# Rows of 1/rms written and spread from ScalarE's queue, and group 0's q in halves

## The chip, the cores and the metric

The kernel runs on one core of a Trainium2 chip. A core has five engines that run beside each other: TensorE (PE, with its weight loads listed apart as PEld), VectorE (DVE), ScalarE (ACT), GpSimd (POOL) and SyncE (SP). SyncE computes nothing here; it issues DMA transfers. ScalarE and GpSimd can issue them too. Each engine works through its own instructions in the order of the program, and waits where an instruction needs the result of another engine or of a transfer.

The metric is the device time of one execution in microseconds (us). Before the change its median was 531.6 us over 3 runs (530.16 to 532.11). The execution that the profiler recorded has a span of 526.9 us, and all times of single instructions below are counted from the start of that span.

## What is computed

There are two blocks. The first is attention with q and k normalised by their root mean square (8 batches, 12 heads, 448 tokens, 64 elements of a head):

```
q_n = q / sqrt(mean(q*q) + 1e-6) * g_q          # k likewise with g_k
attn = softmax(q_n @ k_n.T / 8);  x = attn @ v
```

The heads are put side by side, so that x has 448 rows of 768 elements in each batch. The second block scores each token by x @ w_gate, takes the 128 best of each batch, runs them through a layer of 1024 (w1, relu, w2), and adds the result, weighted by a sigmoid of the score, to those rows of x.

## The kernel before

**Groups and units.** Four heads of one batch make a group: two pairs c of two heads hh. There are 24 groups, n = 0 to 23, three to a batch. A group's 448 keys are cut into 7 blocks of 64; a group and a block make a unit, 168 in all, so units 7n to 7n + 6 belong to group n. For each unit PE multiplies keys by queries (`scores`, L289), ScalarE takes the exponential (L298), with 1/rms of the keys as its scale, one number for each partition, and PE multiplies the result by v (`values`, L313). DVE and, in the first six groups, GpSimd too add the exponentials up over the blocks (`add_probs`, L329 and L335); PE sums those over the keys (L367) and turns them (L392); DVE inverts them (L394), and PE turns the attention's result to tokens (L410), which DVE scales (L412).

**Where q is normalised.** The queries lie along the free dimension of the scores' right operand qT. So 1/rms of the queries has to be a row, the same on the 64 partitions of a head, before DVE can multiply qT by it (`scale_q`, L248). The way there for group n is:
- `squares` (L207) on ScalarE and `sum_squares` (L214 on DVE, then the power of -1/2 at L217 on GpSimd) give rinv, 14 numbers on each of 128 partitions;
- `rows_out` (L228) writes rinv to DRAM as two rows of 896 numbers, one row for each hh;
- `rows_in` (L239) reads each row back to 64 partitions of the tile bc (two buffers); a partition gets 3584 bytes, and the whole of bc is 448 KB;
- `scale_q` multiplies qT by bc and by the product of the two gains.

Before the change SyncE issues all three transfers, between its loads of q, k, v and weights and its stores of x. The first two groups do not go through DRAM: `scale_q_early` (L260, L268) spreads rinv with small matmuls on PE into two PSUM banks and multiplies from there. The scores have four banks in all, of the same pool.

**What sets the order.** The program lists the work of the engines by hand. A step q has four units. It lists the scores, exponentials and values of its units first, then the work given to its slots 4q to 4q + 3 in two halves, with pieces of the second block and other tasks between the halves. Each engine thus finds its part of a slot behind its part of that step's units. SyncE has no part in the units, and so reaches its slots as early as its own waits allow. `prepare(n, slot)` (L658) gives slots to the way of group n's rows: squares and sums in slot to slot + 3, `rows_out` at slot + 6 or + 7, `rows_in` at slot + 8, + 9 or + 10. Slot is 7n - 20 from group 6 on, and at most 7n - 17 before (0 for group 2, 4 for group 3). `scale_q` is in slot 11 for group 2, 15 for group 3, and from then on 7n - 6.

**The beginning.** `Loads.__init__` issues the first loads (two of tok, one of qT) ahead of a branch that picks this program. tok holds the token-major copies from which squares are taken: for each group one for q and one for k, in loads of 448 KB. While the first of them is on its way, PE does 26 transposes of the identity (L164) whose results nobody reads.

Of the kernel before, what the change touches and what calls it, by code (L numbers as in the profile page):

```python
# [10 lines left out]
F32 = mybir.dt.float32  # L11
I32 = mybir.dt.int32
AF = mybir.ActivationFunctionType
OP = mybir.AluOpType
# [11 lines left out]
class Loads:  # L26


    def __init__(self, nc, pool, qT, kT, vp, tok, g2):
        self.nc, self.pool = nc, pool  # L30
        self.src = {"tok": tok, "qT": qT, "kT": kT, "v": vp}
        self.tiles = {}
        self.groups = tok.shape[1]
        self.gcol = pool.tile([128, 2], F32, name="gcol", bufs=1)
        nc.scalar.dma_start(out=self.gcol, in_=g2)
        neg_half = pool.tile([128, 1], F32, name="neg_half", bufs=1)
        nc.vector.memset(neg_half, -0.5)

        warm = pool.tile([128, 1], F32, name="warm", bufs=1)
        nc.scalar.activation(out=warm, in_=neg_half, func=AF.Exp)  # L40
        self.neg_half = neg_half
        self.load("tok", 0, 0)
        self.load("tok", 0, 1)
        self.load("qT", 0)

    def load(self, name, n, i=None):
        b, g = divmod(n, self.groups)
        src = self.src[name]
        if i is not None:
            src = src[b, g, :, i]  # L50
        elif name == "v":
            src = src[b, g]
        else:
            src = src[b, 2 * g : 2 * g + 2].rearrange("c p s -> p c s")
        pool = self.v_pool if name == "v" else self.pool
        bufs = {"tok": 6, "qT": 4, "kT": 3, "v": 3}[name]
        held = [key for key in self.tiles if key[0] == name]
        if len(held) == bufs:
            del self.tiles[held[0]]
        t = pool.tile(list(src.shape), F32, name=name, bufs=bufs)  # L60
        self.nc.sync.dma_start(out=t, in_=src)
        self.tiles[name, n, i] = t

    def get(self, name, n, i=None):
        return self.tiles[name, n, i]
# [3 lines left out]
def fast(  # L69
# [21 lines left out]
    nc = tc.nc  # L91

    B, NP, _, S = loads.src["qT"].shape
    CP = 112
    NJ = S // CP
    D = 64
    NI = S // D
# [14 lines left out]
    norm_pool = ctx.enter_context(tc.tile_pool(name="norm", bufs=2))  # L112
# [7 lines left out]
    ps_sc = ctx.enter_context(tc.tile_pool(name="ps_sc", bufs=4, space=PSUM))  # L120
# [20 lines left out]
    load, get, neg_half = loads.load, loads.get, loads.neg_half  # L141

    ident = const.tile([128, 128], F32, name="ident")
# [12 lines left out]
    for c in range(2):  # L156
        nc.vector.memset(pick_pair[D * c : D * (c + 1), c : c + 1], 1.0)
    nc.vector.scalar_tensor_tensor(
        out=gg, in0=loads.gcol[:, 0:1], scalar=scale, in1=loads.gcol[:, 1:2], op0=OP.mult, op1=OP.mult
    )  # L160

    ps = ps_moe.tile([128, 512], F32, tag="moe", name="warm_ps")
    for _ in range(26):
        nc.tensor.transpose(out=ps[:, 0:128], in_=ident, identity=ident)  # L164

    wg = const.tile([CP, DM], F32, name="wg")
# [36 lines left out]
    def squares(n, i):  # L203
        t = get("tok", n, i)
        sq = sqs[(2 * n + i) % 2]
        for h in [slice(0, 1), slice(1, 2)] if (n, i) == (0, 0) else [slice(0, 2)]:
            nc.scalar.activation(out=sq[:, h, :, 0:D], in_=t[:, h], func=AF.Square, scale=scale)  # L207
        sss[n, i] = norm_pool.tile([128, 2, NI], F32, name="ss", bufs=4)
        return sq

    def sum_squares(n, i, sq):
        ss = sss.pop((n, i))
        for h in [slice(0, 1), slice(1, 2)] if (n, i) == (0, 0) else [slice(0, 2)]:
            nc.vector.tensor_reduce(out=ss[:, h], in_=sq[:, h], axis=AX.X, op=OP.add)  # L214
        rinv = norm_pool.tile([128, 2, NI], F32, name="rinv", bufs=8)
        flat = "p h i -> p (h i)"
        nc.gpsimd.tensor_tensor(  # L217
            out=rinv.rearrange(flat),
            in0=ss.rearrange(flat),
            in1=neg_half.to_broadcast([128, 2 * NI]),  # L220
            op=OP.pow,
        )
        rinvs[n, i] = rinv

    def rows_out(n):

        rows = dram_pool.tile([2, 2 * S], F32, name="rows", bufs=3)
        nc.sync.dma_start(  # L228
            out=rows.rearrange("h (p i) -> p h i", i=NI), in_=rinvs.pop((n, 0))
        )  # L230
        bcs[n] = rows

    def rows_in(n):

        rows = bcs[n]
        bc = norm_pool.tile([128, 2, S], F32, name="bc")
        for hh in range(2):
            src = rows[hh].rearrange("(c s) -> c s", c=2)
            nc.sync.dma_start(  # L239
                out=bc[D * hh : D * (hh + 1)],  # L240
                in_=dataclasses.replace(src, ap=[[0, D]] + [list(x) for x in src.ap]),
            )
        bcs[n] = bc

    def scale_q(n):
# [6 lines left out]
    def scale_q_early(n):  # L252

        rinv = rinvs.pop((n, 0))
        for c in range(2):
            ps = ps_sc.tile([128, 512], F32, tag="sc", name="sc")
            r = slice(D * c, D * (c + 1))
            for i in range(NI):
                for hh in range(2):
                    nc.tensor.matmul(  # L260
                        out=ps[D * hh : D * (hh + 1), D * i : D * (i + 1)],
                        lhsT=rinv[r, hh, i : i + 1].to_broadcast([D, D]),
                        rhs=ident[r, r],
                        start=True,
                        stop=True,
                    )
            t = get("qT", n)[:, c].rearrange("d (p i) -> d p i", i=NI)
            nc.vector.scalar_tensor_tensor(  # L268
                out=t,
                in0=t,  # L270
                scalar=gg,
                in1=ps[:, 0:S].rearrange("d (i p) -> d p i", i=NI),
                op0=OP.mult,
                op1=OP.mult,
            )
# [145 lines left out]
    gates, parts, rowss, highers, ranks, slots_dram = {}, {}, {}, {}, {}, {}  # L421
# [212 lines left out]
    def at(slot, fn, *args):  # L634
        todo.setdefault(slot, []).append(lambda: fn(*args))
# [22 lines left out]
    def prepare(n, slot):  # L658
        sq = {}
        for i in range(2):  # L660
            at(slot + 2 * i, lambda i=i: sq.setdefault(i, squares(n, i)))
            at(slot + 2 * i + 1, lambda i=i: sum_squares(n, i, sq.pop(i)))

        at(slot + (7 if n > 2 else 6), rows_out, n)
        at(slot + (10 if n > 5 else 9 if n > 2 else 8), rows_in, n)

    for n in range(1, n_groups):
        s0 = NI * n
        if n > 2:
            at(max(s0 - 26, 4 * (n - 3)), load, "tok", n, 0)  # L670
            at(max(s0 - 26, 4 * (n - 3)), load, "tok", n, 1)
        if n > 1:
            at(max(s0 - 13, 2), load, "qT", n)
            at(max(s0 - 11, 2), load, "kT", n)
            at(max(s0 - 11, 2), load, "v", n)
            first = max(s0 - (20 if n > 5 else 17), 0)
            prepare(n, first)
            at(max(s0 - 6, first + 11), scale_q, n)
# [73 lines left out]
    for i in range(2):  # L752
        sum_squares(0, i, squares(0, i))
# [515 lines left out]
def _build(nc, ap, cap, out):  # L1269
    D = ap["g_q"].shape[0]  # L1270
    with tile.TileContext(nc) as tc, ExitStack() as ctx:
        load_pool = ctx.enter_context(tc.tile_pool(name="load", bufs=1))
        with tc.tile_pool(name="bound", bufs=1) as pool:
            g = pool.tile([1, 2, D], F32, name="g")
            nc.sync.dma_start(out=g, in_=ap["g_row"])
            loads = Loads(nc, load_pool, *(ap[n] for n in ("qT", "kT", "vp", "tok", "g2")))


            prod = pool.tile([1, D], F32, name="prod")
            nc.vector.tensor_mul(out=prod, in0=g[:, 0], in1=g[:, 1])  # L1280
            nc.vector.tensor_mul(out=prod, in0=prod, in1=prod)
            top = pool.tile([1, 1], F32, name="top")
            nc.vector.tensor_reduce(out=top, in_=prod, axis=AX.X, op=OP.max)
            small = pool.tile([1, 1], I32, name="small")
            nc.vector.tensor_scalar(
                out=small,
                in0=top,
                scalar1=MAX_SCORE * MAX_SCORE / D,
                scalar2=None,
                op0=OP.is_le,  # L1290
            )
            is_small = nc.values_load(small[0:1, 0:1], min_val=0, max_val=1,
                skip_runtime_bounds_check_because="a comparison gives 0 or 1")
        with tc.If(is_small > 0) as cmp, tc.manual_schedule():
            fast(
                tc, loads, *(ap[n] for n in _INS[5:]), cap, out,
            )
        with cmp.Else():
            general(tc, *(ap[n] for n in _INS), cap, out)
# [45 lines left out]
```

## Time and profile before

| | before |
|---|---|
| time, median of 3 (us) | 531.6 (530.16 to 532.11) |
| span of the profiled execution (us) | 526.9 |
| PE busy | 507.6 us, 96% |
| DVE busy | 334.2 us, 63% |
| ACT busy | 278.1 us, 53% |
| POOL busy | 191.8 us, 36% |
| rows_out: issues, median us from issue to landing | 22 of 7 KB, 5.4 |
| rows_in: issues, median us from issue to landing | 44 of 224 KB, 6.4 |
| DVE waiting for bc | 5.1 us, 3 times |

A line of the timeline has the start and the length in us, the engine (SPq and ACTq for the queue of issues), the line of the kernel, the operation, and out<-in by the program's names; what stands in brackets at its end is how long the engine had been idle before, and what ended that. In the chain of work that ended last each piece has its start, its length, and the engine or transfer that filled it. The busy time of an engine is a mean over stages that differ: ScalarE, for instance, is busy for 15.2 of the 20 us from 40 to 60, and for 57.2 of the 100 us from 150 to 250. A transfer's landing is the time at which its last part has arrived; an issue is the instruction that starts it.

### The profile page before, as it was taken

What the parts mean: (1) busy time and instruction counts of PE and PEld (TensorE: products, weight loads), DVE (VectorE), ACT (ScalarE), POOL (GpSimd) and SP (SyncE); (2) the same over time, 40 slices, a digit from 0 to 9 for tenths busy, and PEclk for the clock granted to TensorE, in tenths of its full rate; (3) what the DMA queues carried; (4) which work ended last, traced back from release to release, by engine and by line L of the source; (5) the groups of instructions that cost most, each with busy time, mean ns of one, the idle gap of its engine ahead of it and who ended that gap; (6) DMA issues with size and microseconds to landing.
All of it is one profiled execution on the core that took longest, in us unless ns stands there. A gap on an engine that the chain in (4) does not pass through costs nothing.

```text
span 526.9 us, 11121 instructions
## 1 busy us (share of the span) xinstructions
PE 507.6 (96%) x4482; PEld 298.8 (57%) x4482; DVE 334.2 (63%) x638; ACT 278.1 (53%) x507; POOL 191.8 (36%) x109
## 2 busy tenths in 40 slices
PE   6999997999999999999999999998999999999995
PEld 5544343565744476546654467644664448659694
DVE  4566879579846896658666787467947487336101
ACT  4886873857644845456644585645463474401100
POOL 4956866623512454132712424304621003002102
PEclk9999998999999999999999999999999999999998
DMA  8968779799764297526846396537542231104100
GB/s 304 382 217 291 244 224 345 251 291 340 200 187 161 82 291 232 163 94 192 260 136 183 87 297 211 159 103 223 195 131 71 70 136 31 31 1 143 53 32 35
DMA packets 43405, 93.21 MB, mean 177 GB/s; under 512 B 11059, under 2 KB 23348, under 8 KB 43346
## 3 DMA queue, kind: packets, MB, share of 16 engines
q1 hardware_dynamic: 39938, 86.11, 52.1%
q0 software_dynamic: 3264, 6.31, 3.5%
q8 instruction: 37, 0.61, 0.5%
q14 instruction: 22, 0.18, 0.1%
q10 hardware_dynamic: 144, 0.00, 0.0%
HBM read 74.93 MB, written 25.35 MB: 190 GB/s over the span
## 4 chain that ended last, share of the span: by engine, by line
PE 89%; DVE 4%; DMA 2%; ACT 2%; issue 2%; POOL 0%; DVEq 0%; SPq 0%; ACTq 0%; POOLq 0%
PE sc L289 24%; PE av L313 22%; PE moe_ps L575 13%; PE moe_ps L595 11%; PE sc L595 4%; PE x_ps L410 4%; PE sc L575 4%; PE den_ps L367 3%; DMA bc<-rows 2%; PE denT_ps L392 1%; ACT p L298 1%; DVE sum L335 1%; PE warm_ps L164 1%; DVE ss L214 1%; DVE x L412 1%
## 5 line engine op out<-in xcount | busy, mean ns | idle before, releaser
L298 ACT ACTIVATE p<-sc,rinv 128x448 f32<-128x448 f32 x336 | 186.6, 642 | 106.3 <-PE sc L289 92.5
L217 POOL TENSOR_TENSOR rinv<-ss,neg_half 128x14 f32<-128x14 f32 x48 | 128.8, 2689 | 198.3 <-DVE ss L214 170.6
L289 PE MATMUL sc<-qT,kT 64*64 64x448 f32 x1344 | 154.8, 549 | 1.1 <-DVE qT L268 0.4
L313 PE MATMUL av<-p,v 64*64 64x448 f32 x1344 | 147.1, 537 | 0.0
L335 DVE TENSOR_TENSOR sum<-sum,p 128x896 f32<-128x896 f32 x101 | 111.6, 1105 | 7.2 <-ACT p L298 0.9
L313 PEld LDWEIGHTS av<-p,v 64*64 64x64 f32 x1344 | 60.1, 133 | 67.6 <-issue 56.9
L289 PEld LDWEIGHTS sc<-qT,kT 64*64 64x64 f32 x1344 | 54.3, 133 | 70.9 <-issue 47.0
L214 DVE TENSOR_REDUCE ss<-sq 128x14 f32<-128x910 f32 (+1 forms) x49 | 52.4, 1074 | 33.9 <-ACT sq L207 33.9
L575 PE MATMUL moe_ps<-xeT,w 128*128 128x128 f32 x576 | 69.3, 277 | 0.0
L575 PEld LDWEIGHTS moe_ps<-xeT,w 128*128 128x128 f32 x576 | 66.2, 192 | 5.3 <-issue 5.3
L595 PE MATMUL moe_ps<-w,hT 128*128 128x384 f32 x176 | 61.3, 491 | 0.4 <-DVE xe L604 0.3
L412 DVE TENSOR_TENSOR x<-x_ps,rden 112x512 f32<-112x512 f32 x48 | 32.8, 690 | 37.2 <-PE x_ps L410 36.4
L506 POOL DMA_INDIRECT selected<-x,rank x32 | 33.6, 1050 | 47.3 <-DVE x L498 39.3
L207 ACT ACTIVATE sq<-tok 128x896 f32<-128x896 f32 (+1 forms) x49 | 46.4, 951 | 5.7 <-DMA tok<-in_tok_dram 3.7
L595 PEld LDWEIGHTS moe_ps<-w,hT 128*128 128x128 f32 x176 | 31.7, 190 | 22.5 <-issue 2.5
L436 DVE SCALAR_TENSOR_TENSOR prod<-x,wg 112x256 f32<-112x256 f32 x96 | 41.5, 432 | 3.0
L614 POOL DMA_INDIRECT out_dram<-xe,row x10 | 11.6, 1164 | 81.1 <-DVE rden L394 47.3
L410 PE MATMUL x_ps<-ident,xT 128*112 128x128 f32 x192 | 29.5, 279 | 3.3 <-DVE rden L394 3.3
L335 DVE TENSOR_TENSOR sum<-p 128x896 f32<-128x896 f32 x24 | 25.9, 1078 | 5.2 <-ACT p L298 5.2
L604 DVE SCALAR_TENSOR_TENSOR xe<-sc,xe 128x384 f32<-128x384 f32 (+1 forms) x6 | 3.3, 550 | 40.6 <-PE sc L595 40.6
L410 PEld LDWEIGHTS x_ps<-ident,xT 128*112 128x112 f32 x192 | 21.8, 135 | 12.6 <-issue 7.7
L248 DVE SCALAR_TENSOR_TENSOR qT<-qT,gg,bc 128x896 f32<-128x896 f32 x22 | 25.2, 1147 | 5.1 <-DMA bc<-rows 5.1
(71 smaller groups left out, 311.0 us busy)
## 6 DMA issues: line engine op xcount, KB each, us to landing
tok<-in_tok_dram SPq DMA_DIRECT2D x48, 448.0 KB, 6.3
qT<-in_qT_dram SPq DMA_DIRECT2D x24, 448.0 KB, 6.2
kT<-in_kT_dram SPq DMA_DIRECT2D x24, 448.0 KB, 7.0
v<-in_vp_dram SPq DMA_DIRECT2D x24, 448.0 KB, 7.7
out_dram<-x SPq DMA_DIRECT2D x8, 1344.0 KB, 7.8
bc<-rows SPq DMA_DIRECT2D x44, 224.0 KB, 6.4
xe<-selected SPq DMA_DIRECT2D x8, 385.0 KB, 3.1
w<-in_moe_w_dram SPq DMA_DIRECT2D x6, 512.0 KB, 6.4
```

The costliest lines, as they stand in the source:

```text
L207: nc.scalar.activation(out=sq[:, h, :, 0:D], in_=t[:, h], func=AF.Square, scale=scale)
L214: nc.vector.tensor_reduce(out=ss[:, h], in_=sq[:, h], axis=AX.X, op=OP.add)
L217: nc.gpsimd.tensor_tensor(out=rinv.rearrange(flat), in0=ss.rearrange(flat), in1=neg_half.to_broadcast([128, 2 * NI]), op=OP.pow,)
L289: nc.tensor.matmul(out=scs[hh][D * c : D * (c + 1), 0:S], lhsT=get("kT", n)[r, c, D * i : D * (i + 1)], rhs=get("qT", n)[r, c, :], start=True,
L298: nc.scalar.activation(out=p[:, hh], in_=scs[hh][:, 0:S], func=AF.Exp, scale=rinvs[n, 1][:, hh, i : i + 1],)
L313: nc.tensor.matmul(out=avs[n][c][D * hh : D * (hh + 1), 0:S], lhsT=get("v", n)[r, hh, i, :], rhs=probs[u][r, hh], start=(i == 0), stop=(i ...
L335: nc.vector.tensor_tensor(out=sums[n], in0=probs.pop(u - 1) if begins else sums[n], in1=probs.pop(u), op=OP.add)
L410: nc.tensor.transpose(out=ps[:CP, j, :], in_=t[:, j, :], identity=ident)
L412: nc.vector.tensor_tensor(out=xs[b][:, :, col : col + 128].rearrange("p j (h d) -> p j h d", d=D), in0=ps[:CP].rearrange("p j (h d) -> p j ...
L436: nc.vector.scalar_tensor_tensor(out=prod, in0=xs[b][:, j, cols], scalar=1.0, in1=wg[:, cols], op0=OP.mult, op1=OP.mult, accum_out=gates[b ...
L575: nc.tensor.matmul(out=ps[:, 128 * i : 128 * i + n], lhsT=w1[:, dc, 128 * (f0 + i) : 128 * (f0 + i + 1)], rhs=xeT[:, dc, :n], start=(dc == 0),
L595: nc.tensor.matmul(out=ps[:n, :width], lhsT=hT[:, fc, :n], rhs=w2[:, fc, cols], start=(fc == 0), stop=(fc == NFC - 1),)
```

## The change

Three things change.

1. `rows_out` and `rows_in` are issued by ScalarE in the place of SyncE, which keeps its queue for the loads and stores. `rows_in` becomes one transfer over both rows in the place of two over one row each. The slots become slot + 6 and slot + 8 for all groups.
2. For group 0's q, the load of tok is cut into two halves by hh, and so is the power at L217; squares and sums were in halves already. `scale_q_early` takes two banks at once and spreads all of hh = 0 first, then all of hh = 1, so that PE can begin with the first half.
3. The warm-up transposes go down from 26 to 11, for the spreading to start earlier.

```diff
-        self.load("tok", 0, 0)
+        self.load("tok", 0, 0, parts=2)
...
-        self.nc.sync.dma_start(out=t, in_=src)
+        w = src.shape[1] // parts
+        for part in range(parts):
+            cols = slice(w * part, w * (part + 1))
+            self.nc.sync.dma_start(out=t[:, cols], in_=src[:, cols])
...
-    for _ in range(26):
+    for _ in range(11):
...
         for h in [slice(0, 1), slice(1, 2)] if (n, i) == (0, 0) else [slice(0, 2)]:
             nc.vector.tensor_reduce(out=ss[:, h], in_=sq[:, h], axis=AX.X, op=OP.add)
-        nc.gpsimd.tensor_tensor(
-            out=rinv.rearrange(flat),
-            in0=ss.rearrange(flat),
-            in1=neg_half.to_broadcast([128, 2 * NI]),
-            op=OP.pow,
-        )
+            nc.gpsimd.tensor_tensor(
+                out=rinv[:, h].rearrange(flat),
+                in0=ss[:, h].rearrange(flat),
+                in1=neg_half.to_broadcast([128, (h.stop - h.start) * NI]),
+                op=OP.pow,
+            )
...
-        nc.sync.dma_start(
+        nc.scalar.dma_start(
             out=rows.rearrange("h (p i) -> p h i", i=NI), in_=rinvs.pop((n, 0))
         )
...
-        for hh in range(2):
-            src = rows[hh].rearrange("(c s) -> c s", c=2)
-            nc.sync.dma_start(
-                out=bc[D * hh : D * (hh + 1)],
-                in_=dataclasses.replace(src, ap=[[0, D]] + [list(x) for x in src.ap]),
-            )
+        (h_step, _), row = [list(x) for x in rows.ap]
+        nc.scalar.dma_start(
+            out=bc.rearrange("d c s -> d (c s)"),
+            in_=dataclasses.replace(rows[:, :], ap=[[h_step, 2], [0, D], row]),
+        )
...
-        for c in range(2):
-            ps = ps_sc.tile([128, 512], F32, tag="sc", name="sc")
-            r = slice(D * c, D * (c + 1))
-            for i in range(NI):
-                for hh in range(2):
+        spreads = [ps_sc.tile([128, 512], F32, tag="sc", name="sc") for _ in range(2)]
+        for hh in range(2):
+            for c, i in [(c, i) for i in range(NI) for c in range(2)]:
+                r = slice(D * c, D * (c + 1))
...
-        at(slot + (7 if n > 2 else 6), rows_out, n)
-        at(slot + (10 if n > 5 else 9 if n > 2 else 8), rows_in, n)
+        at(slot + 6, rows_out, n)
+        at(slot + 8, rows_in, n)
```

More of the change, by code (lines that the diff above doesn't have):

```diff
@@ L41, in __init__, with load @@
         self.neg_half = neg_half
-        self.load("tok", 0, 0)
+        self.load("tok", 0, 0, parts=2)
         self.load("tok", 0, 1)
         self.load("qT", 0)
-    def load(self, name, n, i=None):
+    def load(self, name, n, i=None, parts=1):
         b, g = divmod(n, self.groups)
@@ L212, in sum_squares @@
         ss = sss.pop((n, i))
+        rinv = norm_pool.tile([128, 2, NI], F32, name="rinv", bufs=8)
+        flat = "p h i -> p (h i)"
         for h in [slice(0, 1), slice(1, 2)] if (n, i) == (0, 0) else [slice(0, 2)]:
             nc.vector.tensor_reduce(out=ss[:, h], in_=sq[:, h], axis=AX.X, op=OP.add)
-        rinv = norm_pool.tile([128, 2, NI], F32, name="rinv", bufs=8)
-        flat = "p h i -> p (h i)"
-        nc.gpsimd.tensor_tensor(
-            out=rinv.rearrange(flat),
-            in0=ss.rearrange(flat),
-            in1=neg_half.to_broadcast([128, 2 * NI]),
-            op=OP.pow,
-        )
+            nc.gpsimd.tensor_tensor(
[4 more added lines that the diff above has]
+            )
         rinvs[n, i] = rinv
@@ L254, in scale_q_early @@
         rinv = rinvs.pop((n, 0))
-        for c in range(2):
-            ps = ps_sc.tile([128, 512], F32, tag="sc", name="sc")
-            r = slice(D * c, D * (c + 1))
-            for i in range(NI):
-                for hh in range(2):
[L260 to L266, printed above, removed]
+        spreads = [ps_sc.tile([128, 512], F32, tag="sc", name="sc") for _ in range(2)]
+        for hh in range(2):
+            for c, i in [(c, i) for i in range(NI) for c in range(2)]:
+                r = slice(D * c, D * (c + 1))
+                nc.tensor.matmul(
+                    out=spreads[c][D * hh : D * (hh + 1), D * i : D * (i + 1)],
+                    lhsT=rinv[r, hh, i : i + 1].to_broadcast([D, D]),
+                    rhs=ident[r, r],
+                    start=True,
+                    stop=True,
+                )
+        for c in range(2):
             t = get("qT", n)[:, c].rearrange("d (p i) -> d p i", i=NI)
@@ L271, in scale_q_early @@
                 scalar=gg,
-                in1=ps[:, 0:S].rearrange("d (i p) -> d p i", i=NI),
+                in1=spreads[c][:, 0:S].rearrange("d (i p) -> d p i", i=NI),
                 op0=OP.mult,
```

## The prediction

> **What bounds the kernel now.** I read the page's engine shares first, then the chain, then the stretches, and last the order of time on each queue in the first 100 us.
>
> ```profile
> PE 507.6 (96%) x4482; PEld 298.8 (57%) x4482; DVE 334.2 (63%) x638; ACT 278.1 (53%) x507; POOL 191.8 (36%) x109
> PE 89%; DVE 4%; DMA 2%; ACT 2%; issue 2%; POOL 0%; DVEq 0%; SPq 0%; ACTq 0%; POOLq 0%
> ```
>
> TensorE (PE) is busy for 96% of the span, so the change can remove little: the idle 19 us of PE, and time at a low clock. It can add much: any wait that reaches PE. The stretches (columns: window, length, busy us of PE, PEld, DVE, ACT, POOL, then granted clock, DMA share, GB/s) say where:
>
> ```profile
> 10.00:20.00 10.00, 9.82 (x162) 5.28 (x156) 4.66 (x6) 8.22 (x12) 8.61 (x4) 1.00 1.04 397
> 30.00:40.00 10.00, 10.00 (x115) 4.47 (x115) 6.04 (x4) 7.51 (x15) 6.18 (x3) 1.00 0.78 258
> 80.00:100.00 20.00, 16.50 (x162) 7.34 (x158) 14.49 (x30) 11.22 (x21) 13.80 (x8) 0.91 0.88 291
> 150.00:250.00 100.00, 99.72 (x860) 55.44 (x852) 72.54 (x132) 57.17 (x105) 32.06 (x15) 1.00 0.55 167
> ```
>
> From 10 to 20 us the DMA engines are full (share 1.04). From 30 to 40 PE never rests. Between 80 and 100 it loses 3.5 us and runs at 0.91 of its clock. From 150 on it loses almost nothing. The chain and the order of time name what fills the gap after 80:
>
> ```profile
> 34.98 1.67 PE sc L289 x16
> ...
> 71.35 7.98 DMA bc<-rows
> ...
> 87.26 1.10 PE x_ps L410 x4
> 88.36 2.78 PE sc L289 x16
> ```
>
> The broadcast bc of group 5, queued on SyncE behind a 1344 KB store of out, lands at 79.3. VectorE (DVE) waits 2.35 us for it, the reciprocals of L394 come late, and PE waits 3.27 us at 83.99. Then 16 score matmuls take 2.78 us; at 34.98 as many took 1.67.
>
> The broadcast of group 2 has the least room:
>
> ```profile
> 27.83 1.17 SPq L239 DMA_DIRECT2D bc<-rows  x2
> 31.00 2.29 ACT L298 ACTIVATE p<-sc,rinv 128x448 f32<-128x448 f32 x4
> 32.07 1.15 DVE L248 SCALAR_TENSOR_TENSOR qT<-qT,gg,bc 128x896 f32<-128x896 f32 x1 [2.48 <-DMA bc<-rows]
> 37.96 1.68 PE L289 MATMUL sc<-qT,kT 64*64 64x448 f32 x16
> 41.55 0.26 DVE L394 RECIPROCAL rden<-denT_ps 112x16 f32<-112x16 f32 x1 [3.13 <-PE denT_ps L392]
> ```
>
> It is issued at 27.83 and landed by 32.0; the 16 scores at 37.96 are units 14 and 15, the first of group 2, and read that qT. So 4.7 us separate the end of the multiply (33.2) from its reader.
>
> [...] The old broadcast counts 64 on both sides[...]. The new source pattern is [[h_step, 2], [0, 64], row]: its slowest dimension is 2, the destination's is 128[...]. No run of before has such a pattern. [...] In the trace of before ScalarE's ring carries one 1 KB load. [...] 2.78 against 1.67 us after 3.27 us of idling.
>
> **The change, part by part.**
>
> *First q in halves, pow in halves, 11 warm-ups.* The first tok lands at 4.54 and the first squares run at 4.64. A half can land some 0.7 us earlier, but the memsets that the squares also need end at 4.1, so I take 0.4. The pow of 14 columns takes 2.60 us; its half lies between 1.3 (in proportion) and 2.6 (all fixed). I take 1.4, since an add of 896 columns takes 2.08 on the same engine and so the fixed part is small. Together the last of group 0's pow moves from 9.1 to about 8.2, and the first scores from 11.39 to some 10.3. The warm-ups (26 in 4.97 us, 0.21 each while cold) then end near 7.0, and the first half's spreading fills the hole, so I charge nothing for the clock. But this gain is lost at 20 us: the tok of group 2 that ScalarE squares at 17.62 lands at 17.54, the DMA engines being full, and behind it come the sum (18.68) and the multiplies of L268 (19.70), which free the PSUM banks that the scores of 20.42 need. Those times stay. I take 0 here (ends: 0 and -1.1).
>
> *Issue costs on ScalarE.* 44 issues of 0.4 to 0.5 us (SyncE's: 0.38 and 0.50) come to some 20 us of its queue. From 150 us on ACT is busy 57 of 100 us and its gap between two steps' exponentials is 3.6 to 8 us, so they hide there, as does the wait of rows_in for rows_out. Before that the issue is done while the exponentials already queued still run. I take 0 to 2, value 0.5.
>
> *Moved from SyncE to ScalarE.* SyncE runs ahead of the compute; ScalarE issues in program order, behind the four units' exponentials of its step. Group 2's rows_in is in slot 8, after the exponentials of units 8 to 11, which start at 31.00 and end at 33.3. So it issues near 32.3, not at 27.83.
>
> *One broadcast in the place of two.* [...] At full share the 16 engines moved 397/1.04 = 382 GB/s, 23.9 each: 9.6 us. With the 1.8 us that the tiny ScalarE load of gcol took to land, 11.4 us is the lower end. [...] For group 2, SyncE's loads issued by 31.7 land until 38.3, so some 5 us of their work is in the way: I take 16. The old pair landed within 4.2.
>
> *Group 2:* landed 32.3 + 16 = 48.3, multiplied by 49.5; PE reached it at 38.0: a wait of 11.5 us (6.9 to 16.5), and 1.7 for the clock at half rate over 3.4 us. Sum 13.2. Queued behind the waiting multiply on DVE are three sums (33.14 to 38.4) and L394; DVE idled 3.13 before L394, so they add little.
>
> *Group 3:* rows_in is behind the exponentials of unit 15 (41.3), now near 54.9; landed at about 70. DVE reaches its multiply at 46.94 + 13.2 = 60.1 and waits 10. Behind it is the work up to the sums of 57.04 that PE awaited at 58.19, with only 1.6 us of idling. PE loses 7 (4 to 13).
>
> *Later groups:* group 4's rows_in and multiply lie a whole step apart, which is enough, but its rows_out stands behind the long broadcast on the ring while ScalarE waits for it; this falls in the same time as group 3's wait. Group 5's late broadcast stays as late as now: 68.5 + 12 is 80.5, against 79.3. From group 8 on there are six slots, 11 to 20 us, between rows_in and the multiply; 12 to 16 us fit or miss by little. I take 1.5 for all (ends -3 and +10).
>
> Sum: 0 + 0.5 + 13.2 + 7 + 1.5 = 22, over most of which nothing else is on the path. Hence **about 553 us**.
>
> **The rivals.**
>
> *Two engines, little sharing* (every broadcast in 11.4 us): group 2 costs 6.9 + 1.7, group 3 about 3, the rest nothing: 531.6 + 11.6 = 543. For it: while PE stands still SyncE's loads wait for buffers, so the ring empties. Against: 0.78 and 0.85 share in those stretches.
>
> *Sixteen engines, faster.* If the pattern is spread as the old one was, a broadcast lands in 4 to 5 us. Group 2 is then multiplied by about 38, just in time; group 5's is issued at 68.5, ahead of the store, and DVE gets its 2.35 us back, PE is never cold after 84 (1.76 us: 1.1 on the scores, 0.65 on L410): 531.6 - 4.1 = 527.5. For it: this is the only wait for bc that the chain shows. Against: the leading 2 of the pattern.
>
> *Sixteen engines, but ScalarE waits.* rows_out and rows_in of groups 4, 5 and 6 fall in one step, and ScalarE would wait 2 to 3.5 us for the landing before the next exponentials; PE catches 1 to 2 us of each of three. It cancels the gain: 531.6 - 4.1 + 5 = 532.5.
>
> **How the numbers follow.** Two engines with sharing 0.64, two engines with little 0.22, sixteen and faster 0.08, sixteen and no change 0.06. The likeliest gives 553. The range takes both two-engine cases with their bounds, 538 to 568, and leaves out the two others and a tail. Slower by over 0.5%: both two-engine cases, 0.86. Faster 0.08, same 0.06.
>
> **What would show each step right or wrong.** The landing of bc: 11 us or more says two engines, under 6 sixteen. Then DVE's wait before L248 in groups 2 and 3 (2.48 and 0 now): 10 us or more each; a PE gap of 7 to 16 us near 38 us, a slice with PEclk near 5 after it, and another near 60. The scores of 20.42 should stay within 0.5 us. The stretch from 150 us on should be as long as now; if it is not, waits of ScalarE for its own issues reach PE, and I have placed the cost wrongly. [...]

## The result, and the profile after

The changed kernel takes 598.23 us (594.84 to 599.23, 4 runs), the kernel before 530.88 us (530.03 to 532.11, 4 runs) on the same chip: a ratio of 1.1255, with a 95% interval of 1.1204 to 1.1307. It is 67 us slower where 22 were predicted, and outside the range. The profiled span is 596.6 us against 526.9, 69.7 more.

The lines of the page on the engines' shares and on the chain that ended last, changed kernel:

```profile
PE 524.2 (88%) x4467; PEld 304.8 (51%) x4467; DVE 330.9 (55%) x638; ACT 279.5 (47%) x507; POOL 191.9 (32%) x110
PEclk9997798799598999998999999899999999999999
PE 49%; DVE 2%; DMA 1%; issue 1%; ACT 1%; POOL 0%; ACTq 0%; POOLq 0%; DVEq 0%
```

PE fell from 96% to 88% of the span, and is busy 16.6 us longer with the same work: slices of PEclk stand at 5, 7 and 8, and the mean granted clock is 0.954, where it was 0.994. The chain's shares add up to 54% only, because it could be followed back from the end no further than to 267.9 us; so I read the stretches and the waits in place of it. The stretches, with the columns of before and one window more:

```profile
10.00:20.00 10.00, 8.46 (x112) 4.32 (x112) 3.90 (x5) 7.32 (x12) 8.99 (x4) 1.00 1.04 399
30.00:40.00 10.00, 8.65 (x95) 3.55 (x91) 0.10 (x1) 7.19 (x14) 6.35 (x3) 1.00 0.72 237
40.00:60.00 20.00, 10.28 (x94) 4.57 (x98) 9.18 (x16) 6.10 (x12) 2.85 (x2) 0.74 0.26 78
80.00:100.00 20.00, 16.34 (x162) 7.16 (x158) 11.86 (x23) 12.90 (x23) 12.86 (x6) 0.91 0.60 195
150.00:250.00 100.00, 89.94 (x760) 53.97 (x761) 67.78 (x126) 52.85 (x95) 30.92 (x15) 0.92 0.51 167
```

From 40 to 60 us PE is idle for half of the time and runs at 0.74 of its clock, while the DMA engines, taken together, are busy for a quarter of it (0.26): a transfer is awaited, and bandwidth is not what it lacks. From 150 to 250 us PE loses 10 us, where it lost 0.28 before. The waits, changed kernel (engine and line that waits, what ended the wait, us in all, times, longest):

```profile
DVE qT L250 <- DMA bc<-rows: 71.3, 9, 18.1
PE sc L291 <- ACT p L300: 32.7, 9, 12.0
ACT sq L210 <- DMA bc<-rows: 13.2, 1, 13.2
```

DVE waited 5.1 us for bc before. PE waiting for exponentials, the second line, was not among the waits of before at all. Group 2 in the order of time, changed kernel:

```profile
31.98 1.10 ACTq L241 DMA_DIRECT2D bc<-rows  x1
...
48.24 1.15 DVE L250 SCALAR_TENSOR_TENSOR qT<-qT,gg,bc 128x896 f32<-128x896 f32 x1 [18.14 <-DMA bc<-rows]
...
49.49 3.26 PE L291 MATMUL sc<-qT,kT 64*64 64x448 f32 x16 [10.84 <-issue]
...
54.87 0.26 DVE L396 RECIPROCAL rden<-denT_ps 112x16 f32<-112x16 f32 x1 [2.09 <-PE denT_ps L394]
```

The broadcast is issued at 31.98, and the multiply that reads it starts at 48.24: 16.3 us, where the old pair landed within 4.2. PE stands for 10.84 us and then takes 3.26 us for scores that took 1.68. The granted clock is 1.00 until 42.82 us, 0.50 from there to 53.06 and 1.00 again to 60.

The second kind of loss, at group 6. ScalarE's order of time, changed kernel:

```profile
103.07 0.36 ACTq L231 DMA_DIRECT2D rows<-rinv  x1
103.49 0.21 ACT L472 ACTIVATE parts<-parts 112x8 f32<-112x8 f32 x1
103.60 0.94 ACT L210 ACTIVATE sq<-tok 128x896 f32<-128x896 f32 x1
104.44 0.33 ACT L377 COPY den<-den_ps 128x224 f32<-128x224 f32 x1
112.74 0.51 ACTq L241 DMA_DIRECT2D bc<-rows  x1
113.35 0.95 ACT L210 ACTIVATE sq<-tok 128x896 f32<-128x896 f32 x1 [8.58 <-DMA qT<-in_qT_dram]
114.21 2.19 ACT L300 ACTIVATE p<-sc,rinv 128x448 f32<-128x448 f32 x4
```

Between 104.8 and 112.7 ScalarE does nothing. The instruction at which it stands is `rows_in` (L241), which may not be issued before the rows issued at 103.07 have landed; their last packet (the last piece that a DMA engine moved of them) ends at 112.16. These rows lay behind the broadcast of group 5 in ScalarE's own queue, whose last packet ends at 110.67; the rows of groups 3, 4, 7 and 13 likewise ended 0.1, 2.3, 0.1 and 1.8 us behind the broadcast of the group before. So part of the standing comes from the slow broadcasts themselves. The exponentials of 114.21 queue behind it. PE is idle from 107.46 for 7.42 us. (The name in the bracket is the last event that the profile saw, not the cause.)

All PE gaps of over 0.4 us, without the first 4.7 us of the span, come to 59.3 us, against 5.7 before. I put them down by what ended them: three of 10.84, 9.49 and 3.66 us (at 38.66, 64.37 and 90.45) by a multiply that waited for bc or by the reciprocal behind it, 24.0 us; six of 7.42, 12.01, 3.02, 2.47, 4.57 and 1.08 us by exponentials behind a standing ScalarE, 30.6 us; 2.9 us at the start; the rest is small. The growth of the gaps (53.6) and the 16.6 us that PE is busy longer come to 70.2, near the 69.7 of the span. PE was busy at half clock for 28.7 us, before for 3.3; by my estimate this is some 12.7 of the 16.6 (half of the 25.4 us more at half clock).

### The profile page after: what moved, and what is told of

It reads as the page before. It is cut to its first block, busy times and chain, and to the rows that moved or that the text cites. A ratio compares the mean times of both kernels' runs of the same rounds, so it can differ in the third digit from the quotient of the medians.

```text
span 596.6 us, 11076 instructions
## 1 busy us (share of the span) xinstructions
PE 524.2 (88%) x4467; PEld 304.8 (51%) x4467; DVE 330.9 (55%) x638; ACT 279.5 (47%) x507; POOL 191.9 (32%) x110
## 4 chain that ended last, share of the span: by engine, by line
PE 49%; DVE 2%; DMA 1%; issue 1%; ACT 1%; POOL 0%; ACTq 0%; POOLq 0%; DVEq 0%
PE sc L291 12%; PE av L315 11%; PE moe_ps L597 8%; PE moe_ps L577 7%; PE sc L597 4%; PE sc L577 3%; PE x_ps L412 2%; DMA rows<-rinv 1%; PE den_ps L369 1%; PE denT_ps L394 1%; ACT p L300 0%; DMA out_dram<-xe,row 0%; DVE x L414 0%; DVE sum L337 0%; DVE ss L219 0%
## 5 line engine op out<-in xcount | busy, mean ns | idle before, releaser
L220 POOL TENSOR_TENSOR rinv<-ss,neg_half 128x14 f32<-128x14 f32 (+1 forms) x49 | 129.8, 2652 | 267.9 <-DVE ss L219 223.2
L291 PE MATMUL sc<-qT,kT 64*64 64x448 f32 x1344 | 169.2, 581 | 45.5 <-ACT p L300 32.7
L315 PE MATMUL av<-p,v 64*64 64x448 f32 x1344 | 152.6, 543 | 0.0
L291 PEld LDWEIGHTS sc<-qT,kT 64*64 64x64 f32 x1344 | 57.8, 139 | 124.5 <-issue 59.0
L337 DVE TENSOR_TENSOR sum<-sum,p 128x896 f32<-128x896 f32 x101 | 109.9, 1088 | 9.7 <-ACT p L300 3.5
L315 PEld LDWEIGHTS av<-p,v 64*64 64x64 f32 x1344 | 64.8, 136 | 68.6 <-issue 57.3
L250 DVE SCALAR_TENSOR_TENSOR qT<-qT,gg,bc 128x896 f32<-128x896 f32 x22 | 25.3, 1148 | 71.3 <-DMA bc<-rows 71.3
L210 ACT ACTIVATE sq<-tok 128x896 f32<-128x896 f32 (+1 forms) x49 | 46.4, 950 | 38.7 <-DMA bc<-rows 13.2
L412 PE MATMUL x_ps<-ident,xT 128*112 128x128 f32 x192 | 30.1, 282 | 13.4 <-DVE rden L396 13.1
L616 POOL DMA_INDIRECT out_dram<-xe,row x10 | 11.6, 1163 | 83.3 <-DVE rden L396 47.3
L412 PEld LDWEIGHTS x_ps<-ident,xT 128*112 128x112 f32 x192 | 22.1, 136 | 22.8 <-DVE rden L396 13.8
L344 ACT COPY xT<-av 128x448 f32<-128x448 f32 x48 | 23.4, 549 | 9.1 <-PE av L315 8.6
```

The lines of the kernel that those rows point to most:

```text
L220: nc.gpsimd.tensor_tensor(out=rinv[:, h].rearrange(flat), in0=ss[:, h].rearrange(flat), in1=neg_half.to_broadcast([128, (h.stop - h.start) ...
L291: nc.tensor.matmul(out=scs[hh][D * c : D * (c + 1), 0:S], lhsT=get("kT", n)[r, c, D * i : D * (i + 1)], rhs=get("qT", n)[r, c, :], start=True,
L315: nc.tensor.matmul(out=avs[n][c][D * hh : D * (hh + 1), 0:S], lhsT=get("v", n)[r, hh, i, :], rhs=probs[u][r, hh], start=(i == 0), stop=(i ...
L337: nc.vector.tensor_tensor(out=sums[n], in0=probs.pop(u - 1) if begins else sums[n], in1=probs.pop(u), op=OP.add)
L412: nc.tensor.transpose(out=ps[:CP, j, :], in_=t[:, j, :], identity=ident)
```

## The experiments

Theory after this reading: two causes. **Shape:** the one transfer with the leading 2 moves slowly (16.3 us to the multiply of group 2, where the old pair landed within 4.2) and is late at the multiply. **Queue:** ScalarE, which has the exponentials to do, stands at issues that wait. The rivals are that one of the two explains all, or that the new slots do. Ratios are to the kernel before on the same chip.

**Old transfers on ScalarE** (`e1_two_act`: the changed kernel with the pair of 64 rows).

```diff
-        nc.scalar.dma_start(out=bc.rearrange("d c s -> d (c s)"), in_=...[[h_step, 2], [0, D], row])
+        for hh in range(2):
+            src = rows[hh].rearrange("(c s) -> c s", c=2)
+            nc.scalar.dma_start(out=bc[D * hh : D * (hh + 1)], in_=...[[0, D]] + src.ap)
```

> The changed kernel with rows_in as the two transfers of before (64 equal rows on each side), still on ScalarE's queue and in the new slots. Shape theory ([...] nearly all of the 67 us come from its 13 to 18 us of moving): bc lands 4 to 6 us after its issue, and the time is 527 to 537. Queue theory (issuing and waiting in ScalarE's order costs most): 570 to 600, with bc still waited for or ScalarE standing at its issues.

Measured: 557.51 us (554.23 to 562.05), ratio 1.0490 (1.0462 to 1.0518). Neither theory's range held: the shape explains 40 us of the 67, and 27 stay with broadcasts that are fast. The page's chain by line names what replaced them, the landing of rows with 7% of the span; before it had no such entry:

```profile
PE sc L292 21%; PE av L316 19%; PE moe_ps L578 11%; PE moe_ps L598 10%; DMA rows<-rinv 7%; PE sc L598 4%; PE sc L578 3%; PE x_ps L413 3%; PE den_ps L370 2%; POOL rinv L220 2%; DMA bc<-rows 2%; ACT p L301 1%; DMA tok<-in_tok_dram 1%; DMA v<-in_vp_dram 1%; PE denT_ps L395 1%
```

ScalarE's order of time at group 6, in this kernel:

```profile
82.80 0.37 ACTq L231 DMA_DIRECT2D rows<-rinv  x1
83.22 0.96 ACT L210 ACTIVATE sq<-tok 128x896 f32<-128x896 f32 x1 [0.45 <-DMA bc<-rows]
84.08 0.32 ACT L378 COPY den<-den_ps 128x224 f32<-128x224 f32 x1
89.50 1.11 ACTq L242 DMA_DIRECT2D bc<-rows  x2
90.66 0.95 ACT L210 ACTIVATE sq<-tok 128x896 f32<-128x896 f32 x1 [6.26 <-issue]
91.52 2.19 ACT L301 ACTIVATE p<-sc,rinv 128x448 f32<-128x448 f32 x4
```

The same picture as in the changed kernel: ScalarE stands for 5.1 us at `rows_in`, the last packet of the rows ends at 88.20, and PE has a gap of 5.65 us at 86.53. It happens at seven groups (4, 5, 6, 9, 13, 18 and 21), where both issues fall into one step with little of ScalarE's work between them: 2.0 to 5.1 us each, 26.4 in all, each ending 0.5 to 1.3 us after the last packet of the rows. That the queue matters is shown; that it is the standing, and not any issue on ScalarE, was still open.

**The one transfer on SyncE, nothing else changed** (`e2_one_sp`).

```diff
-            nc.sync.dma_start(out=bc[D * hh : D * (hh + 1)], in_=...)        # for hh in range(2)
+        nc.sync.dma_start(out=bc.rearrange("d c s -> d (c s)"), in_=...[[h_step, 2], [0, D], row])
```

> The kernel before with only this changed: rows_in is the one transfer with the leading 2, on SyncE, in the old slots. Shape theory: bc takes 11 us or more from issue to landing and the time is 555 to 600[...]. Queue theory: 529 to 535, as before.

Measured: 574.24 us (2 runs), ratio 1.0826 (1.0804 to 1.0848), inside what the shape theory expected. The shape alone, in the old slots, costs 44 us. Its line among the waits:

```profile
DVE qT L247 <- DMA bc<-rows: 70.5, 10, 12.2
```

That is the 71.3 us of the changed kernel again, without rows or broadcasts on ScalarE.

**The parts of the first group alone** (`e3_first_only`: halves of the load and of the power, 11 warm-ups, the new order of spreading, on the kernel before).

> The kernel before with only the part for group 0: tok in halves, the power in halves, spreading by hh, 11 warm-ups. Both theories: no effect beyond 0.5%, 529.5 to 532.5, first scores near 10.4 us in the place of 11.4 and the scores of 20.4 us within 0.6 of where they were, since the tok of group 2 bounds them. If the head start is kept, 529.8 or less; if the cooler clock costs, over 532.5.

Measured: 530.28 us against 530.24, ratio 1.0000 (0.9991 to 1.0009). These parts do nothing to the time.

**The one transfer on SyncE, rows_out left on ScalarE** (`e4_one_in_sp`: of the changed kernel only the engine of `rows_in` differs, nc.sync for nc.scalar).

> The changed kernel with rows_in (the one transfer) on SyncE, rows_out still on ScalarE, new slots. ScalarE then never waits for a landing. If the loss beyond group 3 comes from ScalarE standing at rows_in for rows_out, and at rows_out for a semaphore that the long broadcast holds, it falls by the PE gaps of the changed kernel that ended on ScalarE (about 30 us with their cold clock): 560 to 575. If it comes from DVE waiting for bc, it stays at 590 or more. Queue theory: about 530 to 540.

Measured: 572.85 us (2 runs), ratio 1.0800 (1.0779 to 1.0821). Taking `rows_in` off ScalarE gives back 25 of the 67 us, about what the queue cost by itself in the first experiment.

**Standing or issuing?** Two kernels with fast pairs. In `e5_next_step` both stay on ScalarE, but `rows_in` waits for the next step, so that exponentials lie between; in `e6_two_in_sp` only `rows_out` is ScalarE's.

```diff
# e5, against e1
-        at(slot + 8, rows_in, n)
+        at((slot + 6) // 4 * 4 + 4, rows_in, n)
# e6, against e1
-            nc.scalar.dma_start(     # in rows_in
+            nc.sync.dma_start(
```

> The changed kernel with rows_in as the two old transfers of 64 rows, both kinds on ScalarE's queue, and rows_in put into the first slots of the step after the one with rows_out, so that four units of exponentials always stand between the two on ScalarE. Theory 'landing': the 27 us that the two-transfer kernel on ScalarE lost (557.5) are ScalarE standing at rows_in for the landing of rows, 4.5 to 8.3 us at some ten groups whose two issues fell into one step, with PE waiting for the exponentials behind. Then this kernel takes 531 to 538 us (2 to 3 us at group 2 stay, which is not moved), and no wait of a score for p over 1 us is left. Rival 'queue': any issue or semaphore wait on ScalarE's queue, wherever it stands, costs the exponentials; then 550 to 558 us.

> The changed kernel with rows_in as the two old transfers of 64 rows on SyncE's queue, rows_out on ScalarE's, slots of the change. ScalarE then never waits for a landing of rows; it can wait only for GpSimd's power at rows_out. Theory 'landing': 531 to 537 us. Rival 'queue': rows_out alone on ScalarE keeps half of the loss, 541 to 547 us. A second rival, 'slots': the earlier slots cost on whichever queue, then about 557 us.

Measured: 536.27 us (535.67 to 538.28) and 530.15 us (528.06 to 530.68) against 528.95; ratios 1.0145 (1.0128 to 1.0162) and 1.0016 (0.9999 to 1.0033). With the same 66 issues on ScalarE, the first gets back 20 of the 27 us just by giving ScalarE work ahead of the wait, and the second, a little under the expected 531, gets back all but 1. What is left of its waits for exponentials:

```profile
PE sc L292 <- ACT p L301: 6.8, 3, 4.7
```

They were 22.3 us, 7 times, in the kernel with both in one step. So it is the standing; an issue by itself took ScalarE 0.37 us for the rows and 1.11 us for a pair (the lines of `e1_two_act` above). The 4.7 us that stay, at 83.21, come from two waits: ScalarE stood from 78.8 at the second broadcast of group 5, issued at 80.28, and from 80.7 at `rows_out` of group 6, issued at 84.88, though the data of both were there (below, under the wait that no run took apart). I had expected no such wait above 1 us; that part of the expectation failed.

**The slots alone** (`e7_slots_only`: the kernel before with slot + 6 and slot + 8 for all groups).

> The kernel before with the slots of the change alone (rows_out at +6, rows_in at +8 for all groups), both on SyncE in the old two transfers. Theory 'landing': SyncE stands for the landing in ScalarE's place and holds only loads that are early, so 529 to 534 us. Rival 'slots': the earlier slots themselves are the loss on any queue, 545 to 557 us.

Measured: 524.77 us (524.60 to 524.97), ratio 0.9921 (0.9908 to 0.9934): faster than the kernel before, and under the expected interval. It is the best of all kernels here. Its page:

```profile
PE 506.3 (97%) x4482; PEld 298.9 (57%) x4482; DVE 334.0 (64%) x638; ACT 277.4 (53%) x507; POOL 192.0 (37%) x109
PEclk9999999999999999999999999999999999999999
```

and SyncE's queue around group 5:

```profile
61.15 0.38 SPq L228 DMA_DIRECT2D rows<-rinv  x1
61.57 1.53 SPq L194 DMA_DIRECT2D w<-in_moe_w_dram  x1
67.34 1.34 SPq L239 DMA_DIRECT2D bc<-rows  x2
69.73 0.69 SPq L424 DMA_DIRECT2D out_dram<-x  x1
```

The broadcast of group 5 is now ahead of the store (L424), and issued at 67.34 in the place of 70.83. DVE's wait for it and the half clock after 84 us are gone, and PE's 3.27 us there are down to 1.29. SyncE stands for the rows here as ScalarE did (56.9 us in all), but the loads queued behind it come in time: ScalarE's squares wait 3.7 us for tok, as in the kernel before. `e6_two_in_sp`, with the same slots and pairs but rows_out on ScalarE, took 5.4 us more on the same chip; no run takes that apart.

**Group 5 alone** (`e8_group5`: rows_out of group 5 in slot + 6, rows_in in slot + 7, all else as before).

> The kernel before with group 5's rows_out one slot and its rows_in two slots earlier (+6 and +7), so that both are ahead of the store of x (slot 26) on SyncE's queue. The only wait of the kernel before for bc that reached PE after the start, 3.27 us at 84 us and 3.4 us at half clock behind it, should go: 526 to 529 us. If the next wait in line (the gates or the store, now later) takes its place, 530 to 532 us.

Measured: 527.33 us (525.75 to 528.35) against 528.95, ratio 0.9968 (0.9954 to 0.9982). That is inside the expected 526 to 529. DVE's wait for bc of group 5 goes here too, and PE's gap at 84 us is 1.28. But a new gap of 1.31 us shows at 115.0, behind DVE: groups 6 and 7, whose slots are the old ones, wait there 2.4 and 4.9 us for bc. With the slots moved for all groups neither those waits nor that gap is there.

**The leading size or the number of transfers?** (`e9_two_lead2`: the kernel with the slots alone, each broadcast in two transfers by columns, each still with a leading 2.)

```diff
+        for c in range(2):
+            src = rows[:, S * c : S * (c + 1)]
+            nc.sync.dma_start(out=bc[:, c], in_=...[[h_step, 2], [0, D], [1, S]])
```

> The kernel with the slots of the change alone (524.8 us, all on SyncE's queue), but each broadcast in two transfers split by columns, so that each of the two still reads with a leading size of 2 (2 rows by 64 copies by 448 numbers, 1792 bytes a piece). Theory 'leading size': it is the leading size of 2, not the number of transfers[...]; then a broadcast again takes 12 to 20 us, at most about 2 of its packets are under way at any time per transfer, and the kernel takes 550 to 580 us. Rival 'number of transfers': two transfers spread as the old two did, 524 to 528 us.

Measured: 577.35 us (2 runs), ratio 1.0916 (1.0889 to 1.0943). Two transfers, each with the leading 2, cost 48 us; two with a leading 64, in the same slots and on the same queue, are the kernel of 524.8. The number of transfers is out. The packets say the same. Counted from the start and end of each 3584-byte packet of bc on ScalarE's queue (2816 of them in either kernel):

```
                       one under way   two      three or more   packet time in all
changed kernel          66.8 us       177.4 us    6.9 us         442.6 us
old pairs on ScalarE     8.3 us         4.1 us   57 us           587.0 us   (up to 19 at once)
```

**The changed kernel with rows_in in the next step** (`e10_one_next_step`: the edit of `e5_next_step` on the kernel with the one transfer).

> The changed kernel with rows_in in the first slots of the step after rows_out, and nothing else altered (one transfer with a leading size of 2, ScalarE's queue). It takes the standing of ScalarE at rows_in away and leaves the slow broadcast. If the two causes add as they did so far (two transfers on ScalarE: 557.5 to 536.3 with this edit), 574 to 582 us. Rival: the slow broadcasts alone hold this kernel, or hold ScalarE through semaphores that they keep, and the edit brings under 8 us: 590 to 598.

Measured: 600.38 us (598.17 to 601.50), ratio 1.1346 (1.1319 to 1.1374). No gain at all: here the two causes do not add. The waits show the exchange:

```profile
DVE qT L250 <- DMA bc<-rows: 118.0, 18, 19.4
PE sc L291 <- issue: 28.0, 2, 17.4
PE sc L291 <- ACT p L300: 10.5, 2, 9.3
```

PE's wait for exponentials fell from 32.7 to 10.5 us, but DVE's for bc rose from 71.3 to 118.0 (the second line is PE behind two of these multiplies): a broadcast that lands 11.6 to 23.5 us after its issue, and is issued up to a step later, is late for its multiply. The fast pairs, with a median of 4.5 us on ScalarE's queue, had the room.

**The one transfer on SyncE in the new slots, and the same prepared earlier** (`e12_one_sp_new`, `e11_earlier`).

```diff
# e11, against e12
-            at(max(s0 - 26, 4 * (n - 3)), load, "tok", n, ...)
+            at(max(s0 - (30 if n > 5 else 26), 4 * (n - 3)), load, "tok", n, ...)
-            first = max(s0 - (20 if n > 5 else 17), 0)
+            first = max(s0 - (24 if n > 5 else 17), 0)
```

> The kernel with the slots of the change alone (524.8 us), but rows_in as the one transfer with a leading size of 2, on SyncE. This is the shape by itself in the slots of the change. Theory 'lateness': a broadcast of 13 to 18 us costs only where it lands after the multiply is due, and the earlier slots give it two slots more than in the kernel with the old slots (574.2), so 562 to 573 us. Rival 'load': the slow broadcast costs by itself, in whatever slot, then 570 to 576.

> The same kernel with the preparation of the groups after the fifth (load of tok, squares, sums, rows_out, rows_in) four slots earlier, and the multiply where it was, so that the slow broadcast has some 10 us more. Theory 'lateness': what groups 2 to 5 lose (30.7 us in the kernel with the old slots) stays, what the groups after them lose (14.5 us there) goes, so 10 to 15 us under the kernel without this edit: 550 to 560 us, and no wait of a multiply for bc over 1 us after group 7. Rival 'load': within 3 us of the kernel without this edit.

Measured: 581.83 us, ratio 1.0980 (1.0925 to 1.1036), and 608.53 us, ratio 1.1484 (1.1440 to 1.1528). Both expectations fell. (Part of what `e11_earlier` computes is wrong, for a reason that is not known, so its time and its waits count for little.) DVE's wait for bc did end there after group 6, as the theory of lateness had it, and yet the kernel was not faster. SyncE's queue of `e12_one_sp_new` points to the reason:

```profile
SPq L238 <- DMA rows<-rinv: 169.7, 22, 11.2
```

In the kernel with the slots alone this wait is 56.9 us in 13 times. The rows' last packet came 13.0 us after the issue (median), against 5.3 with the old pairs. But the wait by itself is not the loss: in `e6_two_in_sp` SyncE stood for the rows 138.6 us in 19 times, and that kernel took 530.15. What costs is what lies behind a slow broadcast in the same queue. SyncE and ScalarE around the broadcast of group 7, in `e12_one_sp_new`:

```profile
131.81 0.52 SPq L238 DMA_DIRECT2D bc<-rows  x1
132.42 0.89 SPq L61 DMA_DIRECT2D tok<-in_tok_dram  x2
...
147.30 0.95 ACT L207 ACTIVATE sq<-tok 128x896 f32<-128x896 f32 x1 [10.40 <-DMA tok<-in_tok_dram]
```

The broadcast landed at 146.08, and the first tok, issued right behind it, at 147.22: 14.8 us after its issue, where the median with the slots alone is 6.2. ScalarE's squares stood for it, the exponentials behind them, and PE was idle for 9.25 us from 139.57. The squares wait 42.8 us for tok in this kernel, and 94.8 in the one with the earlier preparation, where the kernel before has 3.7. So a slow broadcast costs in a third place, at the loads behind it. PE's gaps in `e12_one_sp_new` divide into 24.3 us behind multiplies that waited for bc, or behind the reciprocals after them, and 17.5 us behind squares that waited for tok. In the old slots (`e2_one_sp`) none is of the second kind.

## Why the prediction was wrong

**What held.** (1) The first group's parts: 0 predicted, 0.0 measured. First scores at 10.35 (10.3 predicted), the scores of 20.42 at 20.93, just at the bound of 0.5 us. (2) Few packets at a time: at most two of the broadcasts' packets were under way for 97% of the time in which any was (66.8 and 177.4 of 251.1 us). That the one transfer, for its leading 2, moves on two of the 16 DMA engines was my assumption; no run of before showed it, and no trace here shows the engine of a packet. (3) The landing: 16 us taken for group 2, 16.3 measured to the multiply; over the nine groups at which DVE waited for it 15.8 to 22.8, and 11.1 at the fastest (11.4 was the lower end, an estimate on that assumption: half of the 448 KB at 23.9 GB/s, the mean of one of the 16 engines from 10 to 20 us before, and 1.8 us). (4) `rows_in` of group 2 near 32.3: 31.98. (5) Group 2: 13.2 us predicted, of which 11.5 as the wait; PE stood 10.84 us, and the first scores of group 2 came 11.5 us later than before. (6) The clock: half of it behind this gap, 3.26 us for 16 scores after 10.84 us of standing. The 1.7 us taken for it were an estimate from the kernel before, where the granted clock was 0.50 from 87.17 to 90.59 us, behind the gap of 3.27 us; here 0.50 lasted for 3.57 us after PE went on at 49.49.

**Group 3** was mis-sized but inside its bounds: 7 us (4 to 13) predicted, 12.6 measured as the further shift of the first scores. The multiply waited 11.1 us (10 predicted); PE stood 9.49 us at L412, and I had let too much of DVE's wait be absorbed.

**The step that failed is "Later groups".** I took 1.5 us for all (-3 to +10); from group 4 on the changed kernel loses another 45.6 (its first scores are 24.1 us late at group 3, 50.3 at group 7, 55.3 from group 8 and 69.7 from group 20 on). The sign that the prediction named for a misplaced cost came true: from 150 to 250 us, where PE had lost 0.28 us, it lost 10. Four of its claims fell:
- *"group 4's rows_in and multiply lie a whole step apart, which is enough"*: bc of group 4 was issued at 73.75 and multiplied at 89.5, with DVE idle for 4.4 us; PE lost 3.66 at 90.45.
- *"while ScalarE waits for it; this falls in the same time as group 3's wait"*: true of group 4 alone, where ScalarE stood for 9.3 us until 73.75 and PE was idle until 73.86 anyway. I looked no further. ScalarE stood again at `rows_in` for 8.0 us at group 6 and for 4.3, 6.5 and 5.0 us at groups 9, 13 and 18.
- *"Group 5's late broadcast stays as late as now"*: DVE waited 6.1 us for it, 2.35 before, though what PE lost then came through ScalarE's standing at group 6.
- *"From group 8 on"* the multiply was held to be the only reader to watch. The losses at 144.58, 179.98, 265.49 and 372.20 (22.1 us) came through ScalarE, not through the multiply.

**Behind it stands the line on issue costs,** "as does the wait of rows_in for rows_out": I let a gap of 3.6 to 8 us between two steps' exponentials hide it and charged 0.5 us. With fast broadcasts the queue costs 27 us (557.5), and 7 of them are left where exponentials are put between the two issues. In that gap the wait is not beside other work but in front of it. The landing was mis-sized too: I assumed 2 to 3.5 us in the rival *Sixteen engines, but ScalarE waits*, and only for groups 4, 5 and 6, for 5 us in all. The table of the time before had 5.4 us as the median; with the fast pairs of `e1_two_act` it was 4.5 to 9.0 us from the issue of the rows to that of the broadcast, at seven groups, and the kernel lost 27.

**How the causes combine.** Each against the kernel before on its own chip, the shape is +44 in the old slots and +52 in the new ones (SyncE), ScalarE's queue with fast pairs in the new slots is +27, and both together are +67. But the new slots alone are -4, so in these slots the shape is +56, the queue +31, and both together +72, not 88. That 44 and 27 come near 67 is no law: the causes share part of their loss, and moving `rows_in` a step later gives 20 us back with the fast pairs and costs 4 with the slow broadcast.

**One wait that no run took apart.** At group 8 ScalarE stood from 141.9 to 154.55 at `rows_out`, whose data (the power, done at 136.4) were there. ScalarE around it, changed kernel:

```profile
141.56 0.35 ACT L377 COPY den<-den_ps 128x224 f32<-128x224 f32 x1 [0.91 <-PE den_ps L369]
154.60 0.36 ACTq L231 DMA_DIRECT2D rows<-rinv  x1
155.06 0.95 ACT L210 ACTIVATE sq<-tok 128x896 f32<-128x896 f32 x1 [13.16 <-DMA bc<-rows]
```

By the records the semaphore (the counter by which a landing is told) that it waited for was the one that the broadcast of group 7 counts up, and it went on when that landed, at 154.53. It cost PE 12.01 us; with `rows_in` on SyncE a wait at the same issue cost 9.82. Two waits of `e5_next_step` look the same: a broadcast of group 5 was issued at 80.28, and the store of x, with which it has nothing to do, had landed at 80.26; rows_out of group 6 was issued at 84.88, and a load of qT on SyncE had landed at 84.86. The records name the semaphore of each issue. In the kernel before and in the changed one the transfers of SyncE and ScalarE have eight between them; in the kernel before all 219 take them strictly in turn. In all three waits the semaphore waited for is the one that the issue's own landing counts, last used by the transfer that had just landed. So in these three cases an issue waited for the transfer that used its semaphore last, whatever that carried; the broadcast of group 7, issued at 131.87, kept its semaphore until 154.53, for 22.7 us. That more semaphores would take this loss away was not tried.

## What to carry to other kernels

Before a transfer moves to a compute engine's queue, look up the landing of what it waits for in the table of issues, and ask what that engine has to do next: there the wait stands in front of the work. Either put a step of the engine's own work between issue and wait, or leave the pair on a queue that has nothing urgent behind it. Look at the leading size of a broadcast's access pattern before merging transfers to save issues: here one with a leading 2 took 15.8 to 22.8 us where it was awaited, two with a leading 64 had a median of 6.4 us each. And test the parts one by one: the slots that this change brought are a gain of 0.8% by themselves (0.66 to 0.92%).

## What the runs showed of the hardware that I had not expected

- For the 7 KB of rows, in pieces of 28 bytes, what was ahead in the queue counted for more here than their size. Their last packet left 4.9 us after the issue in the kernel before (median; 2.4 to 7.8), behind loads on SyncE's queue; 2.7 us (1.1 to 8.3) with only the rows on ScalarE's (`e6_two_in_sp`); and 13.0 us (4.1 to 15.8) behind slow broadcasts in `e12_one_sp_new`.
- The broadcasts with the leading 2, of which at most two packets were under way for 97% of their time (changed kernel), held up what lay behind them in their queue: the rows of groups 3, 4, 6, 7 and 13 ended 0.1 to 2.3 us behind the broadcast ahead of them, and in `e12_one_sp_new` a load of tok landed 1.1 us behind that of group 7, 14.8 us after its issue. Loads on the other queue passed it, but slowly: in the changed kernel SyncE's loads of 448 to 512 KB landed 2.2 to 3.8 us apart while the broadcast of group 7 moved on ScalarE's queue (137.96 to 153.16 us), and 1.0 to 1.2 apart once it had landed (154.97 to 158.19).
- An issue whose data were ready stood for 12.7 us (141.9 to 154.55, `rows_out` of group 8): it waited for an unrelated transfer that held its semaphore, and went on 0.02 us after that landed at 154.53. Two issues of `e5_next_step` started 0.02 us after such a landing (80.28 and 84.88).
